# Decay rates of the half blocks: made late on ScalarE behind a switch of activation tables, or early in four separate operations

## The chip, the cores and the metric

The kernel runs on one core of one Trainium2 chip. The metric is the time of one execution on the device, in microseconds (us), lower is better. Every profile here is one execution, and its span is the time from the first to the last instruction on the core.

## What is computed

A decayed linear attention over 4 batches, 8 heads, 768 positions and 64 channels, and behind it a feed-forward layer with Silu. Cut to what matters:

```python
Dmask = np.where(rel >= 0, lam[:, None, None] ** rel[None, :, :], 0.0)
for b in range(nb):
    intra = np.einsum('bhic,bhjc->bhij', qb, kb) * Dmask[None]
    intra = np.einsum('bhij,bhjd->bhid', intra, vb)
    inter = np.einsum('bhid,bhde->bhie', qb * lam_pow[None], kv_state)
    out[:, :, sl] = intra + inter
    kb_dec = kb * rev_pow[None]
    kv_state = lam_block[None, :, None, None] * kv_state + np.einsum('bhsd,bhse->bhde', kb_dec, vb)

h = x @ w_in                            # x: 3072 x 512, w_in: 512 x 2048
g = h * (1.0 / (1.0 + np.exp(-h)))      # Silu
return (g @ w_out).astype(np.float32)
```

All powers of lam are made on the chip as exp(power * ln lam), so the kernel needs Ln and Exp from one activation table of ScalarE and Silu from another.

## The kernel before, in words

**Tiling.** The 3072 rows are 24 blocks of 128 positions (u = 0 to 23), six for each batch, which pass a state from one to the next. Blocks 0 to 14 are handled whole by `attention(u)`, blocks 15 to 23 by `attention_by_halves(u)`, which splits a block in two halves of 64 positions. For each block: q and k are multiplied with powers of lam on VectorE (`qs`, `ks` or `kp`), turned (on TensorE into `tr_ps` and copied by ScalarE or VectorE into `qT` and `kTz` for the early blocks, by DMA for the later ones), multiplied with each other (`st_ps`, L512), masked on VectorE (`st_sb`, L521), and multiplied with `vz`, a copy of v (`x_ps`, L550). Then the result is copied into `xt`. The state is made from `d_ps`: `y` (L628), and on GpSimd `Xz` and `Xf` (L264).

**Feed-forward.** The blocks are put together in groups: [0, 1], [2], [3], [4], [5], [6, 7] and pairs from there on. `first_product` multiplies a group's `xt` with `w_in_bf` (L871) and takes Silu of it on ScalarE (L880) into `g`; `second_product` multiplies `g` with `w_out_bf` (L899) and stores. The first product of a group can be run in pieces: each piece of 512 columns of `w_in` needs two of the eight casts of `w_in` (`cast["i", j]`, L261, VectorE), and each cast needs its load of 512 KB (L329, issued by SyncE, SP). SP issues the early loads one after the other in a fixed list (`order`): q, k and v of blocks 0 to 2, weights 0 and 1, k and v of block 3, weights 2 to 5, q, k and v of block 4, weights 6 and 7.

**Order.** The order of instructions on every engine is made while the kernel is built: `Plan` is a list scheduler. Each operation is given a length for each engine that may do it, the operations that it waits for, a priority (a lower number goes first), and at times a due time `at` ahead of which it isn't placed. The planner repeatedly takes the operation that can start first; among those within 0.02 us of the first, the one of lowest priority number. Where TensorE would be idle early on, it puts in filler products (`warm_ps`, L977). On the chip each engine then runs its own list in that order and waits on semaphores.

**The lines in question.** Ahead of the plan, ScalarE loads the table of Ln and Exp (L158), and makes `log_lam` (L214) and the decay rates of whole blocks (L216 to L223). `neg_h`, the four columns of powers of the halves, is made on GpSimd (L209). The rates of the halves, `lam_bwd_h`, are made by the function `tables` (L653 to L657), which is one operation of the plan, with a length of 1.2, priority 0 and due time 20.0. Its only reader is the product on VectorE at L694 in `attention_by_halves`. The load of the Silu table is an operation of its own (L858, priority 11), which waits for `xt` of block 0. The planner gives a length to that load, and none to loads that are put in where a function is not in the table that is loaded.

Of the kernel before, what the change touches and what calls it, by code (L numbers as in the profile page):

```python
# [9 lines left out]
AF = mybir.ActivationFunctionType  # L10
# [90 lines left out]
def kernel(  # L101
# [10 lines left out]
    nc = tc.nc  # L112
# [23 lines left out]
    plan = Plan()  # L136
# [69 lines left out]
    for hh in range(2):  # L206
        r = slice(64 * hh, 64 * hh + 64)
# [13 lines left out]
    for hh in range(2):  # L221
        r = slice(64 * hh, 64 * hh + 64)
# [25 lines left out]
    def pace(u):  # L248

        return 0.0 if u < 8 else 57.0 + 6.0 * (u - 8)  # L250
# [35 lines left out]
    for n, (kind, j) in enumerate(order):  # L286
        if kind in "KV":
            u, p = j

            def fn(o, kind=kind, u=u, p=p):  # L290
                b, blk = divmod(u, NB)
                if p == 0:
                    val[kind, u] = regs[o["slots"]["reg"]]
                for hh in range(2):
                    nc.sync.dma_start(
                        out=val[kind, u][64 * hh:64 * hh + 64, p],
                        in_=dict(K=k, V=v)[kind][b, 2 * p + hh, blk * BLK:(blk + NL) * BLK, :].rearrange(
                            "(c s) d -> s c d", c=2 * NL))
# [14 lines left out]
        def fn(o, kind=kind, j=j, tag=tag):  # L313
# [16 lines left out]
            else:  # L330
# [4 lines left out]
        o = plan.op({"SP": us}, [prev], fn, n, alloc=[tag],  # L335
                    at=pace(j) - (7.0 if j < 9 else 9.0) if kind in "kvq" else 0.0)
        o["tag"] = tag
        load[kind, j] = prev = o
    at = {key: n for n, key in enumerate(order)}
# [17 lines left out]
    O = {}  # L357
# [292 lines left out]

        O["vz", u] = (vc, oo, dd)

    def tables(o):  # L653
        for hh in range(2):
            r = slice(64 * hh, 64 * hh + 64)
            for c in range(2):
                nc.scalar.activation(lam_bwd_h[r, :, c], log_lam[r, hh::2], AF.Exp, scale=neg_h[r, c:c + 1])  # L657
    made = plan.op({"ACT": 1.2}, [], tables, 0, at=20.0)

    def attention_by_halves(u):  # L660

        b, blk = divmod(u, NB)
        pr = at["v", u]
        first, last = blk == 0, blk == NB - 1
        lq = load["q", u]
        home = u - (u - XH) % NL
        lk, lv = ([load[kind, (home, p)] for p in range(NP)] for kind in "KV")
        own_k, own_v = lk[0], lv[0]
        late = [plan.op({"NONE": 0.0}, [lq] + lk + lv, lambda o: None, 0, after=2.0, at=pace(u))]
# [3 lines left out]
        def cleared(name, ring, deps):  # L673

            def fn(o):
                val[name, u] = ring[o["slots"][name]]
                (nc.vector if o["eng"] == "DVE" else nc.gpsimd).memset(  # L677
                    val[name, u][:, 0:2 * NP] if name == "kp" else val[name, u], 0.0)
            return plan.op({"POOL": 0.95, "DVE": 0.49}, deps + [O.get(("own", name))], fn, pr, alloc=[name])
# [6 lines left out]
        kz = [cleared("kp", kp_all, late)] if new else []  # L686
        k_own = kz[:1]
        for hh in range(2):
            def fn(o, hh=hh):
                r = slice(64 * hh, 64 * hh + 64)  # L690
                if hh == 0 and not new:
                    val["kp", u] = kp_all[o["slots"]["kp"]]
                t = val["kp", u][:, 0:2 * NP].rearrange("p (a b) (e d) -> p a b e d", b=2, e=2)
                nc.vector.tensor_tensor(  # L694
                    t[r, :, :, hh, :], val["K", home][r, :, cs],
                    lam_bwd_h[r][:, :, :, None].to_broadcast([64, NP, 2, 64]), op=AL.mult)
            kz.append(plan.op({"DVE": 0.7}, [lq, made] + lk + late + kz[-1:], fn, pr,
                              alloc=["kp"] if hh == 0 and not new else [], frees=[(own_k, "reg")] if hh and done else []))
            k_own = k_own or kz[:1]
        k_own[0]["deps"] += [O["own", "kp"]] if ("own", "kp") in O and not new else []  # L700
# [144 lines left out]
    for u in range(NU):  # L845
        n = len(plan.ops)
        (attention if u < XH else attention_by_halves)(u)
        if u >= 8:

            for o in plan.ops[n:]:  # L850
                if "PE" in o["engines"]:
                    o["after"] = 0.8
# [2 lines left out]


    G = {}
    table = plan.op({"ACT": 1.3}, [O["xt", 0]], lambda o: nc.scalar.preload_act_table(AF.Silu), 11)  # L858

    def first_product(g):  # L860
        us = groups[g]
# [151 lines left out]
```

## Time and profile before

| what | value |
|---|---|
| time, median of 3 runs | 220.36 us (219.44 to 220.79) |
| the profiled execution's own time | 221.07 us |
| its span | 219.4 us |
| TensorE (PE) busy | 209.7 us, 96% |
| VectorE (DVE) busy | 122.1 us, 56% |
| ScalarE (ACT) busy | 111.3 us, 51% |
| GpSimd (POOL) busy | 71.7 us, 33% |
| granted TensorE clock, mean | 0.997 |
| read from and written to memory | 27.27 MB and 6.29 MB |

In the profile, PE is TensorE's products and PEld its loads of weights, DVE is VectorE, ACT ScalarE, POOL GpSimd, and SPq the queue in which SyncE issues transfers. A line such as "17.01 0.59 ACT L259 ACTIVATE qT<-tr_ps" gives the start, the length, the engine, the line of the code, the operation, and what it writes and reads. L259 and L261 are a helper's lines, so there it is the tile that tells what is done. What stands in square brackets is the idle time of the engine ahead of the instruction, and what ended it.

### The profile page before, as it was taken

The page shows a single profiled execution, that of the slowest core. Times are in us where ns is not written, and L with a number is a line of the kernel's source. Part 1 is how long each engine was busy: PE and PEld are TensorE (multiplying, and loading weights), DVE is VectorE, ACT ScalarE, POOL GpSimd, SP SyncE. Part 2 cuts the span into 40 slices and gives each one's busy share as a digit, 9 for nine tenths or more (in the row PEclk, how much of TensorE's full clock was granted, in tenths as well). Part 3 has the DMA queues.
Part 4 walks back from the last instruction along what each step waited for, and adds up shares of the span by engine and source line. Part 5 has one row for each costly group of instructions (what it writes and reads, how often), then busy time and mean ns, then how long its engine had stood idle before and what let it go on. Part 6 is the DMA issues. An engine that isn't in the chain of part 4 may idle for free.

```text
span 219.4 us, 4993 instructions
## 1 busy us (share of the span) xinstructions
PE 209.7 (96%) x2032; PEld 150.2 (68%) x2032; DVE 122.1 (56%) x197; ACT 111.3 (51%) x197; POOL 71.7 (33%) x106
## 2 busy tenths in 40 slices
PE   4989799999999999999999999999999999999994
PEld 1756588998774557955965599758759896854453
DVE  6776566688636786535979468089676221012121
ACT  5598677995473224731953177826617663620000
POOL 8664303036004520321723373248636710000000
PEclk9999999999999999999999999999999999999998
DMA  5998999899999989999983998775985300101212
GB/s 125 240 287 234 271 240 295 208 341 409 234 245 202 314 213 208 165 192 192 228 207 96 229 225 167 156 192 150 209 193 123 71 3 0 51 33 62 96 51 96
DMA packets 104214, 39.78 MB, mean 181 GB/s; under 512 B 93696, under 2 KB 97152, under 8 KB 104192
## 3 DMA queue, kind: packets, MB, share of 16 engines
q1 hardware_dynamic: 100496, 33.37, 66.6%
q10 hardware_dynamic: 3696, 6.10, 8.0%
q8 instruction: 16, 0.26, 0.5%
q14 instruction: 6, 0.05, 0.1%
HBM read 27.27 MB, written 6.29 MB: 153 GB/s over the span
## 4 chain that ended last, share of the span: by engine, by line
PE 79%; SPq 9%; DMA 8%; DVE 1%; issue 1%; POOL 0%; ACT 0%
PE o_ps L899 34%; PE h_ps L871 34%; DMA stage<-in_moe_w_in_dram 6%; SPq L322 4%; SPq L329 4%; DMA xt<-x_sb 2%; PE st_ps L512 2%; PE o_ps L939 2%; PE x_ps L550 1%; PE x_ps L832 1%; PE x_ps L831 1%; PE st_ps L743 1%; PE d_ps L612 1%; DVE w_in_bf L261 1%; PE d_ps L768 1%
## 5 line engine op out<-in xcount | busy, mean ns | idle before, releaser
L871 PE MATMUL h_ps<-xt,w_in_bf 128*128 128x256 bf16 (+1 forms) x896 | 92.5, 257 | 1.0 <-DMA xt<-x_sb 0.4
L899 PE MATMUL o_ps<-w_out_bf,g 128*128 128x512 bf16 x368 | 85.1, 379 | 0.0
L871 PEld LDWEIGHTS <-w_in_bf 128*128 128x128 bf16 x896 | 75.0, 98 | 9.8 <-DVE w_in_bf L261 1.3
L880 ACT ACTIVATE g<-h_ps 128x512 bf16<-128x512 f32 x96 | 56.1, 596 | 27.7 <-PE h_ps L871 26.6
L264 POOL TENSOR_TENSOR Xz<-y,lam_blk 64x256 bf16<-64x256 f32 x40 | 33.3, 831 | 83.9 <-DVE y L628 51.9
L899 PEld LDWEIGHTS <-g 128*128 128x128 bf16 x368 | 34.5, 98 | 35.3
L261 DVE COPY o_sb<-o_ps 128x512 f32<-128x512 f32 (+2 forms) x25 | 16.6, 665 | 40.5 <-PE o_ps L899 38.0
L259 ACT ACTIVATE xt<-x_ps 128x512 bf16<-128x512 f32 x19 | 11.3, 594 | 28.9 <-PE x_ps L554 16.9
L521 DVE TENSOR_TENSOR st_sb<-st_ps,mask 128x512 bf16<-128x512 f32 x30 | 19.8, 686 | 6.2 <-PE st_ps L512 5.7
L264 POOL TENSOR_TENSOR Xf<-y,lam_blk 128x256 f32<-128x256 f32 x18 | 16.2, 898 | 1.4
L261 POOL CAST Xz<-y 64x256 bf16<-64x256 f32 x18 | 9.9, 550 | 18.6 <-PE x_ps L831 9.9
L694 DVE TENSOR_TENSOR kp<-stage,lam_bwd_h 64x512 bf16<-64x512 f32 x18 | 14.3, 795 | 0.9 <-DMA kTz<-kp 0.6
L749 DVE TENSOR_TENSOR st_sb<-st_ps,mask_h 128x512 bf16<-128x512 f32 x9 | 6.2, 688 | 14.2 <-PE st_ps L743 14.2
L512 PE MATMUL st_ps<-qT,kTz 128*128 128x128 bf16 x120 | 10.9, 225 | 1.3 <-ACT kTz L259 0.8
L259 ACT ACTIVATE o_sb<-o_ps 128x128 f32<-128x128 f32 x1 | 0.3, 278 | 23.1 <-DVE o_sb L261 23.1
L512 PEld LDWEIGHTS <-kTz 128*128 128x128 bf16 x120 | 8.4, 101 | 4.5 <-ACT kTz L259 1.3
L628 DVE TENSOR_TENSOR y<-d_ps,Xf 64x256 f32<-64x256 f32 (+1 forms) x17 | 7.2, 421 | 5.4 <-PE d_ps L612 3.8
L259 ACT ACTIVATE vz<-stage 64x512 bf16<-64x512 f32 x15 | 9.4, 626 | 1.1 <-DVE vz L677 0.9
L261 DVE CAST w_in_bf<-stage 128x1024 bf16<-128x1024 f32 x8 | 6.1, 759 | 6.7 <-DMA stage<-in_moe_w_in_dram 6.7
L259 ACT ACTIVATE kTz<-tr_ps 64x512 bf16<-64x512 bf16 (+1 forms) x11 | 8.2, 746 | 2.3 <-PE tr_ps L464 2.2
L977 PE MATMUL warm_ps<-zeros 128*128 128x512 bf16 x24 | 8.0, 452 | 1.3 <-DVE pos L166 1.3
L704 DVE TENSOR_TENSOR kp<-qf,lam_fwd 128x512 bf16<-128x512 f32 x9 | 6.9, 768 | 3.5 <-DMA qf<-in_q_dram 3.3
(91 smaller groups left out, 193.3 us busy)
## 6 DMA issues: line engine op xcount, KB each, us to landing
qf<-in_q_dram SPq DMA_DIRECT2D x18, 256.0 KB, 4.1
out_dram<-o_sb ACTq DMA_DIRECT2D x17, 256.0 KB, 2.4
stage<-in_moe_w_in_dram SPq DMA_DIRECT2D x8, 512.0 KB, 6.9
stage<-in_moe_w_out_dram SPq DMA_DIRECT2D x8, 512.0 KB, 7.3
kf<-in_k_dram SPq DMA_DIRECT2D x15, 256.0 KB, 5.5
vf<-in_v_dram SPq DMA_DIRECT2D x15, 256.0 KB, 5.1
stage<-in_k_dram SPq DMA_DIRECT2D x24, 96.0 KB, 3.0
stage<-in_v_dram SPq DMA_DIRECT2D x24, 96.0 KB, 2.8
```

What stands on the lines that cost most here:

```text
L259: nc.scalar.activation(dst, src, AF.Copy)
L261: (nc.vector if o["eng"] == "DVE" else nc.gpsimd).tensor_copy(dst, src)
L264: (nc.vector if o["eng"] == "DVE" else nc.gpsimd).tensor_tensor(dst, a, b, op=op)
L322: nc.sync.dma_start(out=t, in_=src[b, :, sl, :].rearrange("h s d -> s h d"))
L329: nc.sync.dma_start(out=t, in_=w_in_r[:, 2 * a:2 * a + 2, m * 512:(m + 1) * 512])
L512: nc.tensor.matmul(val["st", u, half][:, i, :], lhsT=val["kTz", u][:, h // 2, h % 2, :], rhs=qT(h // 2), start=True, stop=True)
L521: nc.vector.tensor_tensor(val["st_sb", u, half], val["st", u, half], m[:, None, :].to_broadcast([128, 4, BLK]), op=AL.mult)
L694: nc.vector.tensor_tensor(t[r, :, :, hh, :], val["K", home][r, :, cs], lam_bwd_h[r][:, :, :, None].to_broadcast([64, NP, 2, 64]), op=AL.mult)
L871: nc.tensor.matmul(t[:, j, :], lhsT=w_in_bf[:, ko, (m * per + j) * 128:(m * per + j + 1) * 128], rhs=xts[g][:, :, ko, :] if turned(us[0]) ...
L880: nc.scalar.activation(t, val["h", g, m], AF.Silu)
L899: nc.tensor.matmul(val["o", u], lhsT=val["g", g, ko][:, i * BLK:(i + 1) * BLK], rhs=w_out_bf[:, ko, :], start=(ko == 0), stop=(ko == KO - 1))
L977: nc.tensor.matmul(t, lhsT=zeros[:, 0:128], rhs=zeros, start=True, stop=True)
```

## The change

The four exponentials of `lam_bwd_h`, one for each pair of half `hh` and column `c`, become four operations of the plan, each with a length of 0.3, priority 10.5 and due time 6.5. The load of the Silu table now also waits for all four. The product that reads `lam_bwd_h` names the four in its list of dependencies. What is computed stays the same.

```diff
-    def tables(o):
-        for hh in range(2):
-            r = slice(64 * hh, 64 * hh + 64)
-            for c in range(2):
+    made = []
+    for hh in range(2):
+        for c in range(2):
+            def fn(o, hh=hh, c=c):
+                r = slice(64 * hh, 64 * hh + 64)
                 nc.scalar.activation(lam_bwd_h[r, :, c], log_lam[r, hh::2], AF.Exp, scale=neg_h[r, c:c + 1])
-    made = plan.op({"ACT": 1.2}, [], tables, 0, at=20.0)
+            made.append(plan.op({"ACT": 0.3}, [], fn, 10.5, at=6.5))
...
-            kz.append(plan.op({"DVE": 0.7}, [lq, made] + lk + late + kz[-1:], fn, pr,
+            kz.append(plan.op({"DVE": 0.7}, [lq] + made + lk + late + kz[-1:], fn, pr,
...
-    table = plan.op({"ACT": 1.3}, [O["xt", 0]], lambda o: nc.scalar.preload_act_table(AF.Silu), 11)
+    table = plan.op({"ACT": 1.3}, [O["xt", 0]] + made, lambda o: nc.scalar.preload_act_table(AF.Silu), 11)
```

## The prediction

> **What bounds the kernel now.** I read the table of busy times first (TensorE 209.7 of 219.4 us), then the chain of waits in order of time, then the timelines of ScalarE and TensorE around the two switches of tables. From 37.32 us to the last product, the chain is almost only TensorE at work: in the windows view TensorE is busy 82.68 of 82.68 us from 37.32 to 120, and 19.48 of 20 from 120 to 140. Ahead of 37.32 the chain is this:
>
> ```profile
> 18.70 1.29 SPq L329
> 20.04 0.47 SPq L329
> 20.55 8.57 DMA stage<-in_moe_w_in_dram
> 29.12 0.02 issue
> 29.14 0.12 DVE w_in_bf L261
> 29.26 5.47 DMA stage<-in_moe_w_in_dram
> 34.73 0.02 issue
> 34.75 0.69 DVE w_in_bf L261
> ...
> 36.40 0.87 DVE w_in_bf L261
> 37.27 0.05 issue
> 37.32 1.70 PE h_ps L871 x14
> ```
>
> The reader is to see that ScalarE isn't in it. The front is set by SP's fixed list of loads: weights 5 land at 29.12, weights 6 at 34.73, weights 7 are cast by 37.27, and only then has TensorE work without end. What ScalarE does there:
>
> ```profile
> 17.01 0.59 ACT L259 ACTIVATE qT<-tr_ps 128x512 bf16<-128x512 bf16 x1
> 17.62 1.28 ACT L657 ACT_TABLE_LOAD   x1
> 18.91 0.99 ACT L657 ACTIVATE lam_bwd_h<-log_lam,neg_h 64x4 f32<-64x4 f32 x4
> 20.37 0.60 ACT L259 ACTIVATE xt<-x_ps 128x512 bf16<-128x512 f32 x1 [0.46 <-PE x_ps L554]
> 20.99 0.63 ACT L259 ACTIVATE vz<-vf 128x512 bf16<-128x512 f32 x1
> 21.64 1.28 ACT L880 ACT_TABLE_LOAD   x1
> 22.93 0.60 ACT L880 ACTIVATE g<-h_ps 128x512 bf16<-128x512 f32 x1
> 23.43 1.02 ACT L259 ACTIVATE kTz<-tr_ps 128x1024 bf16<-128x1024 bf16 x1
> 24.33 1.09 ACT L880 ACTIVATE g<-h_ps 128x512 bf16<-128x512 f32 x2
> 27.20 0.60 ACT L880 ACTIVATE g<-h_ps 128x512 bf16<-128x512 f32 x1 [1.77 <-PE h_ps L871]
> ```
>
> The switch to Exp and the four exponentials end at 19.90, and ScalarE then idles 0.46 us for TensorE. So that first part delays nothing. The switch back to Silu does: it stands ahead of kTz of block 3. But by 27.20 ScalarE has caught up and idles 1.77 us. TensorE in the same stretch:
>
> ```profile
> 24.50 0.62 PE L512 MATMUL st_ps<-qT,kTz 128*128 128x128 bf16 x8 [0.85 <-ACT kTz L259]
> 24.96 0.59 PE L977 MATMUL warm_ps<-zeros 128*128 128x512 bf16 x2
> 25.61 0.38 PE L871 MATMUL h_ps<-xt,w_in_bf 128*128 128x256 bf16 x2
> 26.33 1.70 PE L871 MATMUL h_ps<-xt,w_in_bf 128*128 128x256 bf16 x14 [0.35 <-DVE w_in_bf L261]
> ```
>
> It loses 0.85 us to kTz, does filler, and then waits again, for the cast of weights 3 (25.23 to 26.28 on VectorE, which had itself idled 1.90 us for the load).
>
> **Part by part.** *Removed:* two table loads, 2 x 1.283 = 2.57 us of ScalarE, and the four exponentials from 18.91 to 19.90, 0.99 us. The first load and the exponentials lay in a gap that TensorE ended (0.46 us idle behind them): worth 0 on the path. The second lay on ScalarE's way to kTz of block 3. Without it: Silu at 21.64 in place of 22.93, kTz at 22.14 (0.50 behind, as now; its input tr_ps is there at 21.65), done at 23.16. TensorE is busy until 23.65, so products st_ps start at 23.65 and not at 24.50: the 0.85 us go.
>
> What is late next: filler (0.59) and two products of weights 2 would end near 24.8, and the remaining 14 products still wait for the cast of weights 3, which ends at 26.28. That is VectorE behind a load on SP's list; nothing of ScalarE's releases it. So TensorE resumes at 26.33 as before. At most the cast gets shorter: it took 1.05 us against 0.69 of the same cast elsewhere, with GpSimd's Xf at work from 25.00 to 25.72 beside it, and an earlier Xf could take that away, 0.36 us. The next cover is there for it, too: TensorE's weight loads waited until 29.89 for weights 5, landed at 29.12. And the last one is weights 7, cast by 37.27. Price on the path: 0; bounds: 0 and -1.58 us (all of TensorE's idle time from 23.65 to 37.32, 1.25 + 0.33, if the planner found other work for it). I take 0, as the three casts stand in the chain and ScalarE doesn't.
>
> *Added:* four exponentials at 0.29 us each, 0.23 apart when in a row (0.99 for four). They can't be placed ahead of 6.5 in the planner's time. ScalarE's gaps from there to the Silu load at 12.86 are 8.09 to 8.57 (0.48, ended by y of block 0) and 8.95 to 10.19 (1.24, ended by kTz of block 1): two in the first (0.52) and two in the second (0.52), so y is late by at most 0.05, or by 0.29 if a third goes ahead of it. Behind y wait GpSimd's Xz and Xf of block 1, which end at 11.69; y of block 1 needs Xf at 12.42, for a wait of VectorE on d_ps: 0.7 us of room. Price 0. The wait that is added is on neg_h, which GpSimd ends at 7.31, ahead of 8.09. Bounded from above: if an exponential stood in the gap ahead of kTz of block 0 (5.60 to 6.57), then ScalarE would sit until 7.31, and kTz, qT and y queue behind it, 1.73 us late with four of them; the rows say no, since kTz (priority 2 against 10.5) is ready as that gap ends. From below it can't gain. I take 0.
>
> *Moved:* the Silu load now waits for the four. They end by 10.2 at the latest by these gaps, and the load starts at 12.86 behind qT of block 1: 0. In the planner's list ScalarE has 1.2 us less from its time 20.0 on, which can swap xt of block 2 (20.37) with vz of block 3 (20.99). With vz first and its v there only at 20.97, xt would end at 22.17; its reader starts at 22.59. Price 0, with 0.42 us of room, and TensorE's idle 1.25 us behind that. SP's loads are tied to one another in their list, so none of them moves; in this stretch the list of DMAs, and what they wait for, is as before.
>
> The rows speak on one rule. Both removed loads took 1.283 us, and the activation behind each starts within 0.01 us (18.91 behind 17.62 + 1.28, 22.93 behind 21.64 + 1.28). The Trainium skill (ScalarE: Activation LUTs, "What ACT_TABLE_LOAD costs") gives 1283 ns for a load and some 1380 ns of draining, 2.66 us for each switch, so 5.3 us for two. By that rule, the trace agrees on the load and shows no drain here.
>
> *Sum:* 0 on the path. The profiled execution took 221.07 us (219.4 of span and 1.7 around it), 0.7 above the median; with nothing taken from it, the forecast is the median itself, less a little for the shorter cast: **220.3 us**.
>
> **Rivals.**
>
> *A, the switches are paid in full.* TensorE's queue would pass the whole of ScalarE's time on: 220.36 - 2.57 = 217.8. For it: the 0.85 us wait on kTz is real, and it stands in TensorE's list. Against it: the 0.46 and 1.77 us idle behind the two switches, and the chain. The rule above, paid in full, would give 220.4 - 5.3 = 215.0. Chance 0.05.
>
> *B, part of the front is gained.* If VectorE's masks of block 3 (26.20) come to stand ahead of the cast of weights 3, x_ps of block 3 (0.67 us) fills the hole in front of 26.33. Then TensorE has that much less to do behind 37.32: -0.67, up to the -1.58 above: 219.7 to 218.8. For it: VectorE idles 1.90 us just there, and st_ps will be ready at about 24.1. Against it: the planner never counted these two loads, so in its own time the order there need not change. Chance 0.10.
>
> *C, slower: the order shifts further back.* At 125.19 TensorE waits 0.41 us for `xt<-x_sb`, a transposing transfer that SP issues at 120.78 and that lands 4.36 us later; SP has a transfer for kTz of 1.72 us at 122.72 and loads of 1.49 us at 124.49 right behind. If the new list puts them ahead of it, the end moves by 1.7 us, or by 3.2 with both: 222.1 or 223.6. It decides at once, since no reserve is left there. For it: everything in the plan hangs on the times before it. Against it: the planner's change is 1.2 us of ScalarE at 20, and ScalarE idles for L871's products 50 times, 26.6 us in all, so a shift of its list dies out long before 120. Chance 0.11, half of it over 1%.
>
> *D, the change doesn't do what it says.* If a load were still put in for Exp or Silu, nothing would be removed: 220.4. The exponentials need the table that L158 loads, and copies run under both tables in the trace without a load, so I give it 0.02.
>
> **How the numbers follow.** The forecast of no change has 0.72, D 0.02 with the same time. About 1% (2.2 us) is what a measurement of this kernel can tell from no change. Faster by over 1%: A's 0.05, and 0.02 for B together with an earlier cast of weights 7: 0.07. Slower by over 1%: half of C, 0.055, and 0.025 taken from the forecast's case for a displaced wait that I can't see: 0.08. Same: the rest, 0.85. The range takes the runs shown (219.44 to 220.79 around 220.36), B down to 219.0 and C's first step nearly whole: 218.9 to 221.6. That leaves out A, the second half of C and a tail of B.
>
> **What would show it.** In the profile of the changed kernel: two table loads on ScalarE and not four; the four exponentials between 8.0 and 10.2; st_ps of block 3 near 23.6 without a wait on kTz; the 14 products of L871 still released by the cast of weights 3 near 26.3; weights 7 cast near 37.3 and TensorE full from there. It would be wrong if weights 3 or 7 are cast earlier by more than 0.5 us, if x_ps of block 3 runs ahead of 26.3, or if TensorE's idle time behind 37.3 grows beyond 0.5 us.

## The result

The changed kernel takes 219.07 us (median of 20 runs, 218.42 to 220.64), the kernel before 219.68 us in the same session (20 runs, 219.12 to 221.54): ratio 0.9965, 95% interval 0.9949 to 0.9981. By the ratio that is 0.77 us less (0.42 to 1.12), by the two medians 0.61 us: a small gain that is clear of zero and within the 1% that the prediction called no change.

Apart from the exponentials and the two table loads, the order of instructions changed in three places and nowhere else: d_ps of block 3 now stands ahead of the second product of w_in on TensorE, y ahead of the cast of weights 2 on VectorE, and v's copy of block 3 ahead of xt of block 2 on ScalarE.

### The profile page after: what moved, and what is told of

It reads as the page before. It is cut to its first block, busy times and chain, and to the rows that moved or that the text cites. A ratio compares the mean times of both kernels' runs of the same rounds, so it can differ in the third digit from the quotient of the medians.

```text
span 218.9 us, 4970 instructions
## 1 busy us (share of the span) xinstructions
PE 208.0 (95%) x2012; PEld 150.2 (69%) x2032; DVE 123.4 (56%) x197; ACT 108.5 (50%) x195; POOL 71.3 (33%) x106
## 3 DMA queue, kind: packets, MB, share of 16 engines
q1 hardware_dynamic: 100496, 33.37, 67.5%
## 4 chain that ended last, share of the span: by engine, by line
PE 82%; SPq 8%; DMA 5%; DVE 2%; issue 1%; ACT 1%; POOL 0%; DVEq 0%
PE h_ps L872 36%; PE o_ps L900 34%; SPq L322 4%; SPq L329 3%; DMA stage<-in_moe_w_in_dram 2%; DMA xt<-x_sb 2%; PE st_ps L512 2%; PE o_ps L940 2%; PE x_ps L550 1%; PE x_ps L832 1%; DVE w_in_bf L261 1%; PE x_ps L833 1%; PE d_ps L612 1%; PE st_ps L744 1%; PE d_ps L769 1%
## 5 line engine op out<-in xcount | busy, mean ns | idle before, releaser
L900 PE MATMUL o_ps<-w_out_bf,g 128*128 128x512 bf16 x351 | 82.9, 379 | 0.8
L261 POOL CAST Xz<-y 64x256 bf16<-64x256 f32 x18 | 9.2, 513 | 19.4 <-PE x_ps L832 12.5
L259 ACT ACTIVATE vz<-vf 128x512 bf16<-128x512 f32 x9 | 5.6, 626 | 7.7 <-DMA vf<-in_v_dram 7.7
L978 PE MATMUL warm_ps<-zeros 128*128 128x512 bf16 x21 | 7.5, 462 | 1.4 <-DVE pos L166 1.3
```

Of the source, the lines that this page charges most:

```text
L259: nc.scalar.activation(dst, src, AF.Copy)
L261: (nc.vector if o["eng"] == "DVE" else nc.gpsimd).tensor_copy(dst, src)
L900: nc.tensor.matmul(val["o", u], lhsT=val["g", g, ko][:, i * BLK:(i + 1) * BLK], rhs=w_out_bf[:, ko, :], start=(ko == 0), stop=(ko == KO - 1))
L978: nc.tensor.matmul(t, lhsT=zeros[:, 0:128], rhs=zeros, start=True, stop=True)
```

## The profile after

ScalarE's timeline after the change, start and length first:

```profile
8.16 0.49 ACT L658 ACTIVATE lam_bwd_h<-log_lam,neg_h 64x4 f32<-64x4 f32 x2
8.62 0.38 ACT L259 ACTIVATE y<-d_ps 128x256 f32<-128x256 f32 x1
9.03 0.48 ACT L658 ACTIVATE lam_bwd_h<-log_lam,neg_h 64x4 f32<-64x4 f32 x2
...
20.77 0.63 ACT L259 ACTIVATE vz<-vf 128x512 bf16<-128x512 f32 x1 [2.42 <-DMA vf<-in_v_dram]
21.31 0.58 ACT L259 ACTIVATE xt<-x_ps 128x512 bf16<-128x512 f32 x1
21.82 0.60 ACT L881 ACTIVATE g<-h_ps 128x512 bf16<-128x512 f32 x1
22.33 1.02 ACT L259 ACTIVATE kTz<-tr_ps 128x1024 bf16<-128x1024 bf16 x1
```

The exponentials sit two and two around y. No table load stands in front of the first Silu any more, so kTz of block 3 starts at 22.33 where it started at 23.43. TensorE in that stretch, same kernel:

```profile
22.07 0.40 PE L608 MATMUL d_ps<-vz,kp 128*128 128x64 bf16 x8
22.30 1.93 PE L872 MATMUL h_ps<-xt,w_in_bf 128*128 128x256 bf16 x24
24.07 0.61 PE L512 MATMUL st_ps<-qT,kTz 128*128 128x128 bf16 x8
```

The wait of 0.85 us ahead of st_ps is gone. And the chain of waits, same kernel:

```profile
14.56 4.21 SPq L329
18.77 0.04 issue
18.82 5.46 DMA stage<-in_moe_w_in_dram
24.28 0.02 issue
24.30 1.27 DVE w_in_bf L261
25.57 0.05 issue
25.62 1.70 PE h_ps L872 x14
...
34.52 0.43 DVE y L628
34.97 0.43 DVE y L628
...
35.43 0.88 DVE w_in_bf L261
...
119.65 5.07 DMA xt<-x_sb
```

In this execution weights 3 landed at 24.28, 0.9 us earlier than in the first profile of before, though SP issued the loads 0.3 us later (14.56 against 14.27). TensorE reaches the 14 products that need weights 7 at 36.35 against 37.32, 0.97 us earlier; and it gives 0.8 back at xt of blocks 12 and 13:

```profile
124.77 1.92 PE L872 MATMUL h_ps<-xt,w_in_bf 128*128 128x256 bf16 x16 [1.19 <-DMA xt<-x_sb]
```

That wait was 0.41 us before. So two questions were open. Is the gain ScalarE's, though my sum had it hidden behind the landing of weights 3? And is part of it lost at 125 us?

## The experiments

All ratios are against the kernel before, run on the same chip between the runs of the experiment. Three chips were used; the medians of the kernel before were 219.50 us (beside before_again, after_again, order_back and loads_back), 219.68 us (order_back_2, loads_idle and the two xt_first) and 219.53 us (the rest). A ratio is taken over all of these runs and isn't the quotient of two medians.

| run | what it is | median us | lowest us | ratio, 95% interval |
|---|---|---|---|---|
| before_again | before, once more | 219.43 | 218.91 | 0.9996 (0.9979 to 1.0012) |
| after_again | after, once more | 218.58 | 218.40 | 0.9970 (0.9953 to 0.9987) |
| order_back | no switch, old order | 219.35 | 218.51 | 0.9993 (0.9974 to 1.0012) |
| order_back_2 | the same | 219.71 | 218.49 | 0.9980 (0.9955 to 1.0004) |
| loads_back | new order, both switches, extra tile | 220.63 | 219.55 | 1.0062 (1.0033 to 1.0090) |
| loads_back_2 | the same, no extra tile | 218.94 | 218.32 | 0.9987 (0.9961 to 1.0013) |
| plain_work | new order, copies for the second load | 218.99 | 218.39 | 0.9984 (0.9959 to 1.0009) |
| loads_idle | switches near 120 us, extra tile | 220.60 | 219.87 | 1.0028 (1.0001 to 1.0055) |
| loads_idle_2 | the same, no extra tile | 218.85 | 218.37 | 0.9995 (0.9968 to 1.0021) |
| shifted | after, and one unused tile | 220.71 | 219.33 | 1.0049 (1.0027 to 1.0071) |
| xt_first_before | before, xt's transfer earlier | 220.16 | 219.31 | 1.0033 (1.0002 to 1.0064) |
| xt_first_after | after, xt's transfer earlier | 219.49 | 218.30 | 0.9981 (0.9954 to 1.0007) |

**A second look at both kernels.** No edit.

> The kernel before, once more, for a second profile. If the loads land alike in each execution (theory: the change itself made weights 3 land earlier), their cast starts near 25.2 us again and weights 7 are cast near 37.3. If landings scatter from one execution to the next (theory: scatter), the cast of weights 3 starts anywhere from 24.2 to 25.3. The time is that of before, ratio 1.000.

> The changed kernel, once more. Ratio 0.9965 as measured, within 0.002. Theory of the change: cast of weights 3 starts near 24.3 again. Theory of scatter: anywhere from 24.2 to 25.3; if TensorE's hole ahead of the 14 products of weights 3 is then wider, the end moves with it.

The landings scatter, and more than I had allowed: in this execution of the kernel before, weights 3 were cast from 22.89 us on and not from 25.23, and in the second one of the changed kernel from 23.63 and not from 24.30. The chain of waits ahead of st_ps of block 3 in before_again:

```profile
20.49 0.63 ACT vz L259
21.13 0.07 ACT L880
21.20 1.23 issue
22.43 0.60 ACT g L880
23.02 0.92 ACT kTz L259
23.95 0.05 issue
24.00 1.07 PE st_ps L512 x8
```

The load of the Silu table (L880, 21.13 to 22.41, most of it shown as "issue") is now on the chain, with the Silu and kTz behind it. TensorE waited 0.85 us for kTz again, and this time nothing of VectorE held it up behind that:

```profile
24.00 0.62 PE L512 MATMUL st_ps<-qT,kTz 128*128 128x128 bf16 x8 [0.85 <-ACT kTz L259]
24.45 0.38 PE L977 MATMUL warm_ps<-zeros 128*128 128x512 bf16 x1
25.10 1.91 PE L871 MATMUL h_ps<-xt,w_in_bf 128*128 128x256 bf16 x16 [0.27 <-PE st_ps L512]
...
35.58 2.16 PE L871 MATMUL h_ps<-xt,w_in_bf 128*128 128x256 bf16 x16
```

The first profile was of an execution with late loads (221.07 us), this one of an early one (218.91).

The second profile of the changed kernel shows the other side. Its front is early, and yet weights 7 came late; VectorE's timeline there:

```profile
32.64 0.69 DVE L261 CAST w_in_bf<-stage 128x1024 bf16<-128x1024 f32 x1 [1.58 <-DMA stage<-in_moe_w_in_dram]
...
35.89 0.69 DVE L261 CAST w_in_bf<-stage 128x1024 bf16<-128x1024 f32 x1 [1.37 <-DMA stage<-in_moe_w_in_dram]
```

The second line is the cast of weights 7, behind 1.37 us of waiting for its load. TensorE loses 1.25 us to it. So what a load hides differs from one execution to the next. The ratio, 0.9970, is as expected.

**The old order without the switches**, two runs.

```diff
             made.append(plan.op({"ACT": 0.3}, [], fn, 10.5, at=6.5))
+    plan.op({"ACT": 1.2}, [], lambda o: None, 0, at=20.0)
```

> The exponentials early and no switch of tables, but an empty operation of 1.2 us at the planner's time 20.0, so that all engines have the order of before. Theory ScalarE (the second load, which held up kTz of block 3, is what was paid): ratio 0.9965 as for the change, st_ps of block 3 without its wait of 0.85 us. Theory order (the planner's three swaps, d_ps ahead of the second product, y ahead of the cast of weights 2, v's copy ahead of xt): the gain is lost, ratio 1.000.

> The old order without the two switches, once more, since 0.9993 (0.9974 to 1.0012) stands against theory ScalarE and its own profile has the front 0.67 us earlier than the kernel before in a like execution. Theory ScalarE with a second clamp (xt by DMA near 125 us gives part of it back): 0.996 to 0.999, TensorE waits 0.3 to 1.2 us for xt near 125. Theory order: 1.000, and no lead at weights 7.

The empty operation gives every engine exactly the order of before, but for the exponentials and the loads. The wait for kTz is gone in both profiles, and in the first the piece of weights 6 and 7 (16 products, of which the first two need only weights 6) begins at 34.91 against 35.58 in before_again. The lowest times (218.51, 218.49) are near those of the changed kernel and below all 134 runs of the kernel before (218.88 at the least). But the ratios, 0.9993 and 0.9980, lie above 0.9965, and the first is nearer to what theory order expected. Part of it shows in the profiles: the first waits 0.6 us for xt at 125, the second 1.2 us for weights 7 (and not for xt, as expected). Whether the new order itself adds to the gain isn't settled by the times: the intervals of order_back and of the changed kernel overlap. The part on the prediction, below, compares the orders by their profiles.

**The switches back in the new order.** Four more exponentials behind qT of block 2. At first they went into a tile of their own, which lay behind lam_bwd_h (loads_back); then into an area that is free until late (loads_back_2, shown).

```diff
                     copy(o, val["qT", u][:, t], val["trq", u][:, t])
+                    if u == 2 and t == 1:
+                        for hh in range(2):
+                            r = slice(64 * hh, 64 * hh + 64)
+                            for c in range(2):
+                                nc.scalar.activation(xts[11][r, c, 0:4], log_lam[r, hh::2], AF.Exp, scale=neg_h[r, c:c + 1])
```

> The changed kernel with its new order, and four more exponentials into an unused tile behind qT of block 2, so that the switch to Exp and back to Silu returns to its old place (2 x 1.28 us and 0.99 us of ScalarE). Theory ScalarE: the gain is lost, ratio 0.999 to 1.001, and TensorE waits some 0.6 us for kTz of block 3 again. Theory order: the gain stays, ratio 0.9965.

> The changed kernel, its order, with both switches of tables and four exponentials at the old place again, now written into a part of xt of the last group that is free until late, so that no buffer lies elsewhere than in the changed kernel. Theory ScalarE: the second load holds up kTz of block 3 again, best times 0.7 to 1.4 us above the 218.4 to 218.6 of the changed kernel, ratio 0.999 to 1.003. Theory shift of buffers (the 32 bytes of an extra tile made the earlier such kernel slow): 0.999 to 1.000, clearly below 1.0062.

The first gave 1.0062, more than any theory allowed; the experiment with an unused tile, below, says why. Without the extra tile it is 0.9987: between the two kernels, and a little below the 0.999 that was expected at the least. Its lowest time, 218.32 us, was expected 0.7 to 1.4 us above the changed kernel's and is no higher than that (218.40). Its profile has a wait of 0.3 us for kTz, not 0.85, since in the new order ScalarE copies v of block 3 while it would wait for x_ps of block 2. So the times of this kernel don't show that the gain is lost, and its profile shows a smaller loss than I expected.

**Copies in place of the second load.**

```diff
+                if g == 0 and m == 0:
+                    for n, w in ((0, 512), (2, 512), (0, 256)):
+                        nc.scalar.activation(xts[11].rearrange("p a s -> p (a s)")[:, 256 * n:256 * n + w], zeros[:, 0:w], AF.Copy)
                 nc.scalar.activation(t, val["h", g, m], AF.Silu)
```

> The changed kernel with 1.3 us of plain copies on ScalarE in place of the second load, ahead of the first Silu. Theory ScalarE (its time ahead of kTz of block 3 is what was paid, whatever fills it): TensorE waits some 0.5 to 0.8 us for kTz again, best times near 219.2, ratio 0.999 to 1.001. If table loads have a cost of their own, ratio near 0.9965.

ScalarE in its profile, and below it in that of loads_back_2:

```profile
21.00 1.44 ACT L883 ACTIVATE xt<-zeros 128x512 bf16<-128x512 bf16 x3
22.35 0.58 ACT L884 ACTIVATE g<-h_ps 128x512 bf16<-128x512 f32 x1
22.83 1.02 ACT L259 ACTIVATE kTz<-tr_ps 128x1024 bf16<-128x1024 bf16 x1
```

```profile
21.01 1.28 ACT L886 ACT_TABLE_LOAD   x1
22.31 0.60 ACT L886 ACTIVATE g<-h_ps 128x512 bf16<-128x512 f32 x1
22.80 1.02 ACT L259 ACTIVATE kTz<-tr_ps 128x1024 bf16<-128x1024 bf16 x1
```

From the start of the copies or of the load to the Silu it is 1.35 and 1.30 us. kTz starts at 22.83 and 22.80, and the piece of weights 6 and 7 begins at 35.49 and 35.47. In these two profiles copies cost what the load costs: ScalarE's time there, and nothing of the load besides shows. The times say less. The ratios are 0.9984 and 0.9987, both wide; the wait for kTz is 0.3 us and not 0.5 to 0.8, and the lowest time is 218.39 us where some 219.2 was expected. By the Trainium skill (ScalarE: Activation LUTs, "What ACT_TABLE_LOAD costs") some 1.4 us of draining would come on top of the 1283 ns; the trace of loads_back_2 doesn't show it, as the Silu starts 0.02 us behind the end of the load (21.01 + 1.28 to 22.31).

**The switches where ScalarE idles**: the same four exponentials ahead of xt of block 14, first with the extra tile, then without.

```diff
+            if u == 14:
+                for hh in range(2):
...
             copy(o, xts[g][:, :, i * BLK:(i + 1) * BLK], val["x", u])
```

> The changed kernel with the four exponentials done a second time, into an unused tile, near 117 us, where ScalarE idles some 6 us for xt of block 14; both switches of tables return there (2 x 1.28 us). Theory ScalarE (a switch costs by what waits behind it): no cost, ratio 0.9965 to 0.997 as for the change. If loads cost something wherever they stand (a disturbance of transfers): 0.999 to 1.000.

> The changed kernel with the four exponentials and both switches near 120 us, where ScalarE idles, without an extra tile. Theory ScalarE with shift of buffers: 0.9965 to 0.998, as the changed kernel, best times near 218.5. If the loads themselves cost wherever they stand: 1.003 again.

With the tile 1.0028, without it a median of 218.85 and a lowest time of 218.37, like the changed kernel's; the ratio, 0.9995, is above the 0.9965 to 0.998 expected, and its interval (0.9968 to 1.0021) reaches the changed kernel's but also 1.000. So its times alone don't show that the switches are free there. Its profile does: it has the shortest span of all, 216.8 us, with both loads in it (119.32 and 122.33), and shows TensorE in the front without any of the waits named so far:

```profile
21.57 0.40 PE L613 MATMUL d_ps<-vz,kp 128*128 128x64 bf16 x8
21.80 1.93 PE L877 MATMUL h_ps<-xt,w_in_bf 128*128 128x256 bf16 x24
23.57 0.61 PE L512 MATMUL st_ps<-qT,kTz 128*128 128x128 bf16 x8
...
35.14 2.05 PE L877 MATMUL h_ps<-xt,w_in_bf 128*128 128x256 bf16 x15
```

**An unused tile alone.** The changed kernel with one tile of 32 bytes per partition that nothing reads or writes.

```diff
     lam_bwd_h = const.tile([128, NP, 2], F32)
+    unused = const.tile([128, NP, 2], F32)
```

> The changed kernel with one unused tile of 32 bytes per partition behind lam_bwd_h, so that the buffers made after it lie 32 bytes further; no instruction differs. Theory shift of buffers: transfers take longer (share of the DMA engines from 37 to 120 us 1.12 against 0.96 to 1.02), ratio 1.001 to 1.004. Otherwise 0.9965.

The ratio is 1.0049, above the 1.001 to 1.004 expected and some 0.8% above the changed kernel (0.9965), with the same instructions in the same order. That is what made loads_back and loads_idle slow, and the times of neither tell anything of the switches. The profile's part on DMA queues (packets, MB, share of 16 engines), the changed kernel first, then the one with the tile:

```profile
q1 hardware_dynamic: 100496, 33.37, 67.5%
```

```profile
q1 hardware_dynamic: 100496, 33.37, 74.3%
```

**The transfer of xt ahead of others.** In both kernels, the transposing transfer of xt of blocks 12 and 13 was put ahead of one load pair of v and of the transfer of kTz of block 15.

```diff
...
+    late_sp[1] = load["V", (18, 0)]
+    moved = {id(o): n for n, o in enumerate(late_sp[:3])}
+    begin = next(t for t, _, o in seq if o is late_sp[3])
+    seq = sorted(((begin + 0.001 * (1 + moved[id(o)]) if id(o) in moved else t, n, o) for t, n, o in seq), key=lambda x: x[:2])
     for _, _, o in seq:
```

> The kernel before with one change far behind the front: the transposing transfer of xt of blocks 12 and 13 is issued ahead of one load pair of v and of the transfer of kTz of block 15. Theory second clamp: TensorE's wait near 125 us (0 to 0.8 us in the profiles so far) goes; 0.998 to 1.000.

> The changed kernel with the same change. Theory second clamp: the wait near 125 us (1.2 us in the first profile, none in the second) goes, and what the front gained comes through: 0.994 to 0.996, and against the kernel before with the same edit 0.9955 to 0.997. If the front's gain was never given back, 0.9965 to 0.997 as without the edit.

The wait for xt went in both profiles, and no gain came: 1.0033 and 0.9981, both above what was expected. In xt_first_before TensorE waits 2.1 us for kTz of block 15 instead: the transfer that was moved back is late next. So the guess that this point alone holds the gain back didn't bear out. Against each other the two give 0.9948 (0.9981 / 1.0033), close to the 0.9955 to 0.997 expected, but with intervals too wide to say more than that the change gains here too. No kernel tried is shown to be faster than the changed one.

## Why the prediction held, and which step of it failed

*Right.* Two table loads are left; the exponentials run at 8.16 and 9.03, in the two gaps named, and y is late by 0.05 us. v's copy of block 3 went ahead of xt of block 2. st_ps of block 3 no longer waits. The whole is within 1%, and 219.07 lies in the range.

*Luck.* It lies 0.17 us above the lower end, and that end stood there for B, which didn't happen. The forecast of 220.3 is 1.2 us too high: 0.7 of it because the median of three runs (220.36) lay that much above the median of twenty (219.68), the rest because a gain was put at 0.

*The step that failed* is the one behind "What is late next": that the cast of weights 3 brings all of the 0.85 us back, "Price on the path: 0". It was read off one execution, as if it were true of the kernel. How much of the wait reaches the end depends on when the loads land. From the first product of w_in to the first of the piece of weights 6 and 7, with what shows as late on TensorE in between, the profiles have:

| kernel | us | worked out from | late |
|---|---|---|---|
| before, first profile | 16.69 | 36.86 - 20.17 | kTz, weights 3 |
| before_again | 15.91 | 35.58 - 19.67 | kTz |
| xt_first_before | 15.92 | 36.19 - 20.27 | kTz |
| loads_back, loads_back_2 | 15.33 | 36.25 - 20.92, 35.47 - 20.14 | kTz, by less |
| plain_work | 15.18 | 35.49 - 20.31 | kTz, by less |
| after | 15.30 | 35.89 - 20.59 | weights 1 and 3 |
| after_again | 15.20 | 35.01 - 19.81 | v of block 3 |
| xt_first_after | 15.62 | 35.46 - 19.84 | v of block 3 |
| order_back_2 | 15.36 | 35.48 - 20.12 | kp of block 3 |
| order_back, loads_idle_2 | 14.89 | 34.91 - 20.02, 35.14 - 20.25 | nothing |
| shifted, loads_idle | 14.89, 14.90 | 35.78 - 20.89, 35.35 - 20.45 | nothing |

15.91 to 14.89 is 1.02 us where no load interferes. It is more than the 0.85 in the brackets because these count from the end of the product ahead, and products in a row start ahead of that end (st_ps at 23.34 in order_back, against 22.44 + 1.06 = 23.50). By starts, st_ps comes 1.91 us behind the second product in before_again (24.00 - 22.09) and 0.90 us in order_back (23.34 - 22.44), in the same order: 1.01 us.

The table also separates the load from the order. Without the load ahead of kTz, the old order (order_back) and the new one (loads_idle_2) have the same 14.89 us. With both switches, the new order has 15.33 and the old one 15.91: the new order alone is worth 0.58 us in this stretch, since v's copy no longer stands between x_ps and kTz. So there are two ways to the same end, less work of ScalarE just ahead of kTz. The new order isn't free, either. Under *Moved* I priced it at 0 and saw only the swap of v's copy with xt; I didn't see that d_ps of block 3, which reads that copy, moves ahead of the second product of w_in. Where v lands late, TensorE now waits there: some 0.3 us in after_again and 0.7 us in xt_first_after.

From the start of that piece to the end of the span it is 181.6 us in before_again (217.2 - 35.58), 181.6 in loads_back_2 and plain_work and 181.7 in loads_idle_2, so in such executions the front's gain goes through to the end. It is 183.0 in after, 182.8 in after_again, 182.7 in order_back and 182.9 in order_back_2: these lose 1.2 us to weights 7 (after_again, order_back_2), or 1.2 and 0.6 us to xt at 125 (after, order_back). The start of the first product moves as well, from 19.67 to 20.59 us among the kernels without an extra tile, and not visibly by kernel.

So 0.77 us is an average over executions, and only single ones were profiled. That the gain is 0 where weights 3 land as late as in the first profile is still only the prediction's reading; no run shows it. That ScalarE's time ahead of kTz lengthens the front, by about 1 us in the old order, is shown by the profiles. By times alone, the experiments that put it back (0.9987 and 0.9984) don't separate from the changed kernel.

*The rivals.* A, the full 2.57 us, is out: the first switch lay in an idle stretch, as the prediction had it. B came near in size (0.67 us), by another way: no mask was moved, the hole on TensorE simply closed. C named the right place, 125 us, and the wait there did reach 1.19 us; but the order of SP is unchanged, and the kernel is not slower. D is out.

*The signs of being wrong.* In the first profile after the change "if weights 3 or 7 are cast earlier by more than 0.5 us" came true for both (24.30 against 25.23, and 36.31 against 37.27 for the end of weights 7). So did, with the wait of 1.19 us at 125, the idle time of TensorE behind 37.3. The first told of scatter, not of the change: before_again casts weights 3 at 22.89. The third is absent from after_again, which doesn't wait at 125.

## What to carry to other kernels

A wait that one profile shows to be hidden behind a transfer is hidden in that execution. Look at how far the landing moves between executions before its price is put at 0; where the profiled execution lies above the median of the runs, as here, look at the loads first. And an experiment that adds a buffer should not move the others: put its scratch data where nothing behind it shifts.

## What was not expected of the hardware

A tile of 32 bytes per partition that nothing uses, which moves all buffers made after it, raised the share of the load queue on the DMA engines from 67.5% to 74.3% for the same 100496 packets and 33.37 MB, and the time by some 0.8%. The two other kernels with such a tile have 75.2% and 75.7%, their twins without it 66.7% and 66.8%; all eleven profiles without the tile lie from 66.5% to 68.2%. As the kernels are laid out, the buffers that the loads write (`stage`, `qf`, `kf`, `vf`) start at multiples of 256 bytes of a partition without the tile, and 32 bytes behind one with it. The Trainium skill (DMA: Bandwidth & Descriptors, "How a descriptor splits into AXI transactions") says that a descriptor which doesn't start at a multiple of 256 bytes costs additional beats. The measured rise would fit that, if it holds for the side that is written, of which the section says nothing. The share of the queue of the stores, q10, whose buffers moved too, hardly differs (8.6% to 9.2% with the tile, 8.0% to 8.9% without). The addresses were not varied further, so the cause is not shown.
